# Attention and an expert MLP fused on one core: v of granule 1 loaded ahead of w_in, and its head's bias products, masks and scores rearranged

## The chip, the cores and the metric

One core of one Trainium2 chip. The time is the device time of one execution in microseconds (us). A program on one core has no second core to compare with, so a run counts as fast if it is within 1.5% of the fastest run of the same kernel; every run told here that could be classified was fast, at a granted TensorE clock of 0.992 to 1.0 (one experiment has a single run, whose state is unknown). The profile is of one execution; its span is some 2 us shorter than the device time.

Engines: PE = TensorE matmul, PEld = its weight load, DVE = VectorE, ACT = ScalarE, POOL = GpSimd, SP = SyncE.

## The reference, cut to what matters

```python
# q, k, v: (4 batches, 8 heads, 768 positions, 64), float32
scores = q @ k.T / sqrt(64)
keep   = (pos_k < 8) | ((0 <= pos_q - pos_k) & (pos_q - pos_k < 96))   # 8 global keys, window of 96
scores = where(keep, scores - slope[h] * dist, -1e9)
a      = softmax(scores) @ v                        # slope[h] = 2 ** -(h + 1)
x      = a as (3072 tokens, 512)
out    = (s * relu(x @ w_in) ** 2 + b) @ w_out      # w_in 512 x 2048, w_out 2048 x 512
```

## The kernel before: the parts concerned

The tokens are worked off in 12 granules of 256 (j below); three granules make a batch. P1(j, f) is the f-th of eight groups of eight matmuls of x @ w_in. P1(0, f) is the first user of piece f of w_in. S are the scores of a granule, A is attention times values, XT is the transposition of its result for P1. A comment marks what is cut.

A score can get its bias and its mask in two ways. Either PE adds the bias before the scores (SB_mm, one matmul per head with a scaled diagonal as weights, `biased=True`), or DVE multiplies the exponentials by exp(bias) afterwards (S_mul with tmpl). The second way needs ACT to have made tmpl. In the granules 0 and 1 everything goes the first way.

```python
    # all loads are issued by POOL, in this order
    load_v(0)
    load_quads(1, "k")
    load_quads(1, "q")
    load_w_in(0, 8)
    load_w_in(1, 8)
    load_v(1)
    for i in range(2, 8):
        load_w_in(i, 8)
    # ... k, q, v of granule 2, three pieces of w_out; later more_loads():
    #     k of 3, last piece of w_out, q of 3, v of 3, granule 4

    def SB_mm(j, hp, which=None):           # bias on PE
        # ...
        for hi in range(2):
            nc.tensor.matmul(
                ps[:, hi, 0:n], lhsT=diag[:, 2 * hp + hi, :], rhs=m, start=True, stop=False
            )

    def S_mul(j, hp):                       # mask on DVE
        # ...
            m = tmpl[:, 2 * hp : 2 * hp + 2, c0 : c0 + n]
            nc.vector.tensor_tensor(pt[:, :, 0:n], pt[:, :, 0:n], m, ALU.mult)

    # the order of the head, from granule 1 on
    SB_mm(1, 0)
    P1(0, 0, "dve", "pso")
    SB_mm(1, 1)
    S_mm(1, 0, True)
    S_post(1, 0, True)
    S_mm(1, 1, True)
    S_post(1, 1, True)
    P1(0, 1)
    SB_mm(1, 2)
    S_mm(1, 2, True)
    S_post(1, 2, True)
    VO(1)
    SB_mm(1, 3)
    S_mm(1, 3, True)
    S_post(1, 3, True)
    A(1, 0)
    A(1, 1, "pso")
    P1(0, 2)
    make_tmpl(0)
    make_tmpl(1)
    A(1, 2)
    P1(0, 3)
    A(1, 3, "pso")
    XT_half(1, 0, "act", "av")
    P1(0, 4)
    XT_half(1, 1, "dve", "pso")
    P1(0, 5)
    P1(1, 0)                                # from here PE streams
```

The softmax here doesn't subtract the row's maximum and nothing guards it: scores larger than these inputs give would overflow.

## Time and profile before

| | before |
|---|---|
| median of three runs | 208.09 us (208.04 to 208.14) |
| span of the profiled execution (a further one, 207.70 us) | 205.9 us |
| PE busy | 199.9 us, 97% |
| start of P1(0,0), P1(0,1), P1(0,2), P1(0,5) | 12.69, 14.66, 17.89, 21.44 us |
| landing of pieces 0, 1, 2, 5 of w_in | 12.04, 13.38, 17.13, 21.15 us |

A load is done by 16 DMA engines, and its completion comes in 16 parts. It has landed with the last part, and that is the time in the table. One view more is needed for the comparison, PE's timeline of the head (start, duration, instruction, count):

```profile
12.69 1.06 PE L528 MATMUL ps<-xT,w_in_bf 128*128 128x256 bf16 x8
...
14.66 1.05 PE L528 MATMUL ps<-xT,w_in_bf 128*128 128x256 bf16 x8
...
21.44 5.41 PE L528 MATMUL ps<-xT,w_in_bf 128*128 128x256 bf16 x48
```

P1(0,0) starts 0.65 us and P1(0,1) 1.3 us after its piece has landed. PE does not wait for pieces 0 and 1. The third line is the start of the stream, P1(0,5).

### The profile page before, as it was taken

Reading aid. Unit: us, or ns where it says so; the run is one execution under the profiler, and the core shown is the slowest. Engines: PE = TensorE matmul, PEld = TensorE weight load, DVE = VectorE, ACT = ScalarE, POOL = GpSimd, SP = SyncE. Lnnn points to the kernel's source line nnn. Section 1 sums busy time; section 2 is a strip of 40 time slices with the busy share of each in tenths; the row PEclk is TensorE's granted clock in tenths of the full one; section 3 lists DMA queues with packets and bytes.
Section 4 is the critical chain, followed back from the end, with each engine's and each line's share of the span. In section 5 each row is a group of like instructions: output and inputs, shape, how many; then the busy total and the mean of one; then the engine's idle time right before and its main releaser. Section 6 shows DMA issues by size and latency. Waiting matters only on the chain.

```text
span 205.9 us, 5605 instructions
## 1 busy us (share of the span) xinstructions
PE 199.9 (97%) x2291; PEld 161.0 (78%) x2299; DVE 169.1 (82%) x409; ACT 118.3 (57%) x181; POOL 73.7 (36%) x98
## 2 busy tenths in 40 slices
PE   7999999999999999999999999999999999999993
PEld 2667886547766678988988988988978988988883
DVE  3685576799989989788799799788799799787693
ACT  5779799455978586536446546546356446424400
POOL 8994673848273019009019029037000000000000
PEclk9999999999999999999999999999999999999999
DMA  5999999999999979999999969979946040050022
GB/s 165 194 183 198 190 194 193 182 148 162 134 125 155 211 112 102 188 159 129 190 128 106 208 82 117 204 114 119 194 80 178 3 135 21 0 153 3 2 105 102
DMA packets 103962, 27.64 MB, mean 134 GB/s; under 512 B 91392, under 2 KB 102016, under 8 KB 103936
## 3 DMA queue, kind: packets, MB, share of 16 engines
q0 software_dynamic: 70976, 13.11, 85.0%
q1 hardware_dynamic: 31904, 13.64, 34.2%
q10 hardware_dynamic: 1056, 0.52, 0.9%
q8 instruction: 18, 0.29, 0.6%
q14 instruction: 8, 0.07, 0.2%
HBM read 27.26 MB, written 6.29 MB: 163 GB/s over the span
## 4 chain that ended last, share of the span: by engine, by line
PE 83%; DVE 8%; ACT 3%; DMA 3%; issue 1%; POOL 0%; SPq 0%; DVEq 0%; ACTq 0%; POOLq 0%
PE ps L528 37%; PE ps_w L702 14%; PE ps_wb L702 6%; PE ps L589 6%; PE ps_av L446 5%; PE ps_s L395 5%; PE ps_wa L702 4%; ACT pt L408 2%; DMA raw<-in_k_dram 2%; PE ps_s L379 2%; DVE xn L464 2%; PE ps_2s L589 2%; DVE pt L418 2%; DMA xT<-xn 1%; DVE o_pr L627 1%
## 5 line engine op out<-in xcount | busy, mean ns | idle before, releaser
L528 PE MATMUL ps<-xT,w_in_bf 128*128 128x256 bf16 x768 | 96.6, 273 | 0.5 <-DVE xn L464 0.2
L528 PEld LDWEIGHTS <-w_in_bf 128*128 128x128 bf16 x768 | 72.7, 98 | 11.4 <-DVE xn L464 0.5
L540 ACT ACTIVATE gT<-ps 128x512 bf16<-128x512 f32 x72 | 43.1, 598 | 58.7 <-PE ps L528 55.9
L408 ACT ACTIVATE pt<-ps_s 128x1024 bf16<-128x1024 f32 (+1 forms) x48 | 43.1, 952 | 2.4 <-PE ps_s L395 2.4
L702 PEld LDWEIGHTS <-sw 128*128 128x128 bf16 x288 | 28.1, 98 | 3.4
L418 DVE TENSOR_TENSOR pt<-pt,tmpl 128x1024 bf16<-128x1024 bf16 (+1 forms) x40 | 25.1, 646 | 2.8 <-ACT pt L408 2.3
L556 DVE TENSOR_TENSOR gT<-gT 128x512 bf16<-128x512 bf16 x68 | 25.8, 415 | 1.8 <-ACT gT L540 1.6
L112 POOL DMA_DIRECT2D vaug<-in_v_dram x24 | 21.5, 913 | 3.9 <-DMA w_out_bf<-in_moe_w_out_dram 1.7
L702 PEld LDWEIGHTS <-gT 128*128 128x128 bf16 x208 | 19.7, 98 | 3.2 <-issue 0.2
L464 DVE TENSOR_TENSOR xn<-ps_av,rc 128x256 bf16<-128x256 f32 x48 | 20.4, 424 | 1.7
L125 POOL COPY pdum<-xT 1x1 bf16<-1x1 bf16 x5 | 3.0, 595 | 49.3 <-DMA xT<-xn 49.3
L589 PE MATMUL ps<-w_out_bf,gT 128*128 128x512 bf16 x74 | 18.8, 379 | 0.4 <-issue 0.2
L702 PE MATMUL ps_w<-tw,sw 128*128 128x256 bf16 x144 | 18.7, 273 | 0.0
L712 DVE SCALAR_TENSOR_TENSOR u<-ps_w,s_bc,bvec 128x256 f32<-128x256 f32 x27 | 12.9, 478 | 6.3 <-PE ps_w L702 6.3
L446 PEld LDWEIGHTS <-pt 128*128 128x128 bf16 x352 | 15.3, 98 | 3.6 <-DVE pt L418 1.2
L538 ACT ACTIVATE gT<-ps 128x512 bf16<-128x512 f32 x24 | 14.2, 599 | 5.1 <-PE ps L528 5.0
L104 POOL DMA_DIRECT2D qnat<-in_q_dram x18 | 16.0, 906 | 2.7 <-PE ps L528 1.8
L104 POOL DMA_DIRECT2D knat<-in_k_dram x18 | 15.9, 893 | 2.1 <-issue 1.6
L446 PE MATMUL ps_av<-vaug,pt 128*128 128x65 bf16 x224 | 16.4, 194 | 0.3 <-DVE pt L418 0.2
L463 DVE RECIPROCAL rc<-ps_av 128x4 f32<-128x4 f32 x48 | 8.7, 181 | 8.8 <-PE ps_av L446 8.5
L589 PEld LDWEIGHTS <-gT 128*128 128x128 bf16 x96 | 8.8, 98 | 8.1
L395 PE MATMUL ps_s<-qT,kT 64*128 64x128 bf16 x224 | 12.5, 218 | 0.0
(99 smaller groups left out, 240.8 us busy)
## 6 DMA issues: line engine op xcount, KB each, us to landing
out_dram<-o_pr SPq DMA_DIRECT2D x10, 512.0 KB, 5.9
vaug<-in_v_dram POOLq DMA_DIRECT2D x24, 128.0 KB, 7.9
knat<-in_k_dram POOLq DMA_DIRECT2D x22, 128.0 KB, 6.1
qnat<-in_q_dram POOLq DMA_DIRECT2D x22, 128.0 KB, 8.0
w_in_bf<-in_moe_w_in_dram POOLq DMA_DIRECT2D x8, 256.0 KB, 7.9
w_out_bf<-in_moe_w_out_dram POOLq DMA_DIRECT2D x4, 512.0 KB, 10.1
out_dram<-o_pr SPq DMA_DIRECT2D x3, 256.0 KB, 2.6
raw<-in_q_dram ACTq DMA_DIRECT2D x2, 256.0 KB, 4.8
```

Of the source, the lines that this page charges most:

```text
L104: nc.gpsimd.dma_start(t[:, i, :, :], src[b, :, sb * P : (sb + 1) * P, :].rearrange("h p d -> p h d"))
L112: nc.gpsimd.dma_start(vaug[b % 2][:, sb, :, 0:D], v[b, :, sb * P : (sb + 1) * P, :].rearrange("h p d -> p h d"),)
L395: nc.tensor.matmul(ps[:, hi, oc * P : (oc + 1) * P], lhsT=kt[r, :], rhs=qT[j][r, hp, i * P : (i + 1) * P], start=not biased, stop=not bias ...
L408: nc.scalar.activation(pt[:, :, 0:n], ps[:, :, 0:n], ACT.Exp, scale=QSCALE)
L418: nc.vector.tensor_tensor(pt[:, :, 0:n], pt[:, :, 0:n], m, ALU.mult)
L446: nc.tensor.matmul(av[:, i, hi, :], lhsT=pt[:, hi, c * P : (c + 1) * P], rhs=vv, start=n_ == 0, stop=n_ == len(ops) - 1,)
L464: nc.vector.tensor_tensor(xn[j][:, :, 2 * hp : 2 * hp + 2, :], av[:, :, :, 0:D], rc[:].to_broadcast((P, GB, 2, D)), ALU.mult,)
L528: nc.tensor.matmul(ps[:, i, :], lhsT=w_in_bf[:, kc, fc * P : (fc + 1) * P], rhs=xT[j][:, kc, :], start=(kc == 0), stop=(kc == KC - 1),)
L540: nc.scalar.activation(gs.rearrange("p f (r t) -> p f r t", r=2), ps[:].rearrange("p f (t r) -> p f r t", r=2), ACT.Relu,)
L556: nc.vector.tensor_tensor(gs, gs, gs, ALU.mult)
L589: nc.tensor.matmul(po[j, tb], lhsT=gT[j][:, fc, tb * P : (tb + 1) * P], rhs=w_out_bf[:, fc, :], start=(fc == 0), stop=(fc == FC - 1),)
L702: nc.tensor.matmul(wt[j, ps], lhsT=lhs[:, f, :], rhs=rhs[:, f, :], start=first and f == 0, stop=f == HF - 1, skip_group_check=True,)
```

## The change

Its intent, as the code shows it: take two of granule 1's four bias products off PE and put the work on DVE as masks, start granule 1's scores while the first piece of w_in is still under way, and have its v there early. The masks for the repeated block pattern are also made with fewer, longer ACT calls from a smaller table. The diff, cut to its core:

```diff
     load_quads(1, "q")
-    load_w_in(0, 8)
-    load_w_in(1, 8)
     load_v(1)
-    for i in range(2, 8):
+    for i in range(8):
         load_w_in(i, 8)
# ... diag (8 scaled diagonals) goes; bias (8 scaled copies of a 3-block base) comes,
#     and the bias product becomes ident x bias instead of diag x base
-    tmpl = const.tile([P, H, 5 * P], BF16, name="tmpl")
+    tmpl = const.tile([P, H, 3, P], BF16, name="tmpl")
# ... make_tmpl: four calls for several heads instead of eight for one
     def S_mul(j, hp):
+            m = m[:, :, 1:3, :].rearrange("p h a c -> p h (a c)")
+            x = pt[:].rearrange("p h (i c) -> p h i c", i=GB)
+            nc.vector.tensor_tensor(x, x, m.unsqueeze(2).to_broadcast((P, 2, GB, 2 * P)), ALU.mult)
# ... the head, from granule 1's first bias product on
     SB_mm(1, 0)
-    P1(0, 0, "dve", "pso")
-    SB_mm(1, 1)
+    XT_half(0, 1, "dve", "psh")
+    T_ev(1, 1, "q", "act")
+    T_ev(1, 1, "k")
+    KO_own(1)
+    VO(1)
     S_mm(1, 0, True)
     S_post(1, 0, True)
-    S_mm(1, 1, True)
-    S_post(1, 1, True)
-    P1(0, 1)
-    SB_mm(1, 2)
-    S_mm(1, 2, True)
-    S_post(1, 2, True)
-    VO(1)
+    S_mm(1, 1)
+    S_post(1, 1, mul=False)
+    P1(0, 0, "late", "pso", relu="dve")
+    S_mul(1, 1)
+    S_mm(1, 2)
+    S_post(1, 2, mul=False)
+    P1(0, 1, "late", relu="dve")
     SB_mm(1, 3)
     S_mm(1, 3, True)
     S_post(1, 3, True)
-    A(1, 0)
-    A(1, 1, "pso")
-    P1(0, 2)
-    make_tmpl(0)
-    make_tmpl(1)
-    A(1, 2)
-    P1(0, 3)
-    A(1, 3, "pso")
+    S_mul(1, 2)
+    P1(0, 2, "late")
# ... A(1,0), A(1,1), P1(0,3), A(1,2), A(1,3), each normalised apart
     XT_half(1, 0, "act", "av")
-    P1(0, 4)
+    P1(0, 4, "late")
     XT_half(1, 1, "dve", "pso")
+    for f in range(5):
+        Q(0, f)                             # the five squares that were put off
     P1(0, 5)
```

## The prediction

> **What bounds the kernel now.** I read the page first, then the chain that ended last, then the timeline of the first 25 us.
>
> ```profile
> span 205.9 us, 5605 instructions
> PE 199.9 (97%) x2291; PEld 161.0 (78%) x2299; DVE 169.1 (82%) x409; ACT 118.3 (57%) x181; POOL 73.7 (36%) x98
> PE   7999999999999999999999999999999999999993
> PE 83%; DVE 8%; ACT 3%; DMA 3%; issue 1%; POOL 0%; SPq 0%; DVEq 0%; ACTq 0%; POOLq 0%
> ```
>
> PE is 97% busy and carries 83% of the chain. Only the first slice (5.1 us) has idle PE to speak of, yet the change touches almost only the first 35 us. So the question is when PE reaches the point from which it only streams. In the chain in order of time that point is the eight-matmul groups of the first MLP product (L528, called P1(granule, pair) below):
>
> ```profile
> 17.46 0.59 PE ps_av L446 x16
> 18.05 0.87 PE ps L528 x8
> 19.17 0.87 PE ps L528 x8
> 20.51 0.87 PE ps L528 x8
> 21.61 5.24 PE ps L528 x48
> ```
>
> P1(0,2), P1(0,3), P1(0,4) come one by one, then P1(0,5) starts a run of 48. Pair f needs piece f of w_in. When the pieces land is seen on POOL, which issues the loads; it has eight landing semaphores in rotation, so each issue waits for the load issued eight before it:
>
> ```profile
> 6.96 1.51 POOL L129 DMA_DIRECT2D w_in_bf<-in_moe_w_in_dram  x2
> 8.43 1.79 POOL L112 DMA_DIRECT2D vaug<-in_v_dram  x2
> 10.17 4.50 POOL L129 DMA_DIRECT2D w_in_bf<-in_moe_w_in_dram  x6
> ...
> 16.20 0.61 POOL L92 DMA_DIRECT2D knat<-in_k_dram  x1 [0.86 <-DMA vaug<-in_v_dram]
> 17.42 0.61 POOL L92 DMA_DIRECT2D qnat<-in_q_dram  x1 [0.60 <-DMA w_in_bf<-in_moe_w_in_dram]
> 18.80 0.61 POOL L92 DMA_DIRECT2D qnat<-in_q_dram  x1 [0.77 <-DMA w_in_bf<-in_moe_w_in_dram]
> 20.10 0.90 POOL L112 DMA_DIRECT2D vaug<-in_v_dram  x1 [0.69 <-DMA w_in_bf<-in_moe_w_in_dram]
> 21.43 0.88 POOL L112 DMA_DIRECT2D vaug<-in_v_dram  x1 [0.44 <-DMA w_in_bf<-in_moe_w_in_dram]
> ```
>
> The four issues at 17.42, 18.80, 20.10 and 21.43 wait for pieces 2, 3, 4 and 5. Asked one by one for their time to landing (7.0, 7.6, 8.2, 8.8 us, issued 0.73 us apart from 10.17), these pieces land at 17.15, 18.5, 19.8 and 21.15; pieces 0 and 1 at 12.05 and 13.4 (5.1 and 5.7 us after issue). PE starts P1(0,2..5) at 17.9, 19.0, 20.3 and 21.44: it runs only 0.75, 0.5, 0.5 and 0.3 us behind the arrivals. PE looks like the bound here, but w_in stands right behind it.
>
> One more thing delays these arrivals. The DMA view of 13.5 to 14.7 us has
>
> ```profile
> q8 instruction: 1, 0.02, 5.0%
> ```
>
> one instruction fetch: 5.0% of 16 engines over 1.2 us, so 0.96 us of one engine. One sixteenth of every load then comes late: the second v load, due 0.83 us after the first (14.25), is complete only at 15.9, and the pieces behind it inherit some 0.75 us. Eighteen such fetches in the kernel against some 4,600 PE instructions is one in about 256, so a fetch comes at a place in PE's program, not at a time.
>
> **What the Trainium skill says.** "TensorE: Matmul & The Clock Gate", section "Wait — 56ns, not 53.3ns?", gives a warm matmul N / 2.4 GHz + 2.5 ns from start to start: 109 ns for 256 columns, 216 for 512. The trace agrees (0.87 us for 8). "VectorE: DVE Perf Modes", section "What auto-detection actually checks": 16-bit operands with step ±1 take the two-element mode. The mask multiplication of 1024 elements takes 685 ns here, where (1024/2 + 151)/0.96 gives 691; the trace agrees for the old pattern, and an outer stride of zero does not break the stated condition. That the same copy with a repeated source block takes as long (426 against 430 ns, the two copies of vo) supports it. "ScalarE: Activation LUTs", section "What ACT_TABLE_LOAD costs": 186 + 0.833·N ns; the 1024-element exponentials take 1,025 ns (1,039 by that). "DMA: Bandwidth & Descriptors", section "Queues, rings and completion order": an engine takes descriptors of one ring in order. The trace agrees: loads land in the order of issue, so moving the v loads ahead makes two pieces of w_in later by exactly these loads.
>
> **The change, part by part.**
>
> *PE.* Head pairs 1 and 2 of granule 1 lose their bias product: 2 × 2 × 216 ns = 0.87 us. The instruction order shows 4,592 rows instead of 4,600, and the second granule's scores for pairs 0 and 1 now stand before P1(0,0), pair 2 between P1(0,0) and P1(0,1). All else on PE is the same work.
>
> *DVE.* In: two mask multiplications of 0.685, two ReLUs from PSUM of about 0.69 (estimate from the 0.42 us of the 128x256 normalisation, which also reads PSUM), six bias tables of 384 elements, about 0.2 each (estimate from 0.125 for 128). Out: four diagonals (0.50), two base copies. The tables fall into DVE's 1.28 us wait for q before 4.83, and the rest is about 2.7 us between 15 and 18, where DVE now idles 2.2 us. The five late squares merely move to 22 to 25 us, where DVE is half busy. Nothing of this is on the path.
>
> *ACT.* Eight masks of 640 (8 × 0.751) become four calls, two of 1024 and two of 512: 5.6 down to about 3.3 us. One of 1024 goes into ACT's 0.96 us wait before 5.96; about 1.03 long, it delays the first q copy by at most 0.1 us, and PE is still in bias products until 6.6. Off the path.
>
> *Loads.* v of granule 1 before w_in. From the last q load (11.07) to the second v load the stream delivers two pieces of w_in (1.34 us each) and two v loads (0.85 each, of which about 0.97 for the first after q), 4.0 us in all. In the new order piece 1 stands last of these four, so it is due at 15.1, and piece 0 at 13.75. The fetch comes at about the 360th PE row, which after the change is reached about half a microsecond earlier, around 13.1; it hits piece 0. So I take piece 0 at 14.5 and piece 1 at 15.9. Pieces 2 to 7 stay where they are.
>
> *The head of PE anew.* Scores of pairs 0 and 1: q transposed by 11.8, evacuated on ACT by 13.0, so done by 13.35 (before: 14.7). Then P1(0,0) waits for piece 0: 14.5. It ends 15.4; scores of pair 2 with two changes of matmul shape 0.47; P1(0,1) at 15.9, just with piece 1; end 16.8. Bias product 0.44 and scores 0.47 of pair 3: P1(0,2) at 17.75, piece 2 long there. From here before had P1, A, P1, A, transposes, P1, transposes = 3 × 0.87 + 2 × 0.245 + 2 × 0.22 = 3.54 (17.9 + 3.54 = 21.44, as measured). After, all four A (attention times values) stand there: 4.04. P1(0,5) at 17.75 + 4.04 = 21.8, against 21.44. So +0.35 us: the 0.87 us saved on PE, and the earlier scores, turn into a wait of 1.2 us for piece 0. From P1(0,5) on the stream is the same, PE is full to the end, and the shift goes through. Gaps downstream (summing PE starts, under 1 us between 33 and 77) may absorb 0.1.
>
> Sum: 208.09 + 0.35 - 0.1 = 208.3 us.
>
> **Rivals.** (1) The saving comes through. For it: PE has no gaps in the head worth the name after 12.5. Against: P1(0,5) cannot start before piece 5 lands at 21.15, and no load order changes what lies before that piece. That caps the gain at 0.3 us: 207.8. It needs the fetch to come after piece 1. (2) The repeated table drops the mask multiplication to one element a cycle: 28 calls become 1.22 us, 28 × 0.53 = 15 us more on an engine that is busy 169 of 206; perhaps 214 to 218. Against: the skill's condition, and the vo copies. (3) ACT relief shortens 33 to 40 us, where three masks run on ACT before the exponential at 36.59. Against: that exponential waited for PE (0.33 from the scores), and the two remaining masks take as long there; 0.1 us. (4) ReLU and multiplication on DVE make the last two A wait: their masks are done by about 18.2, needed at 20; nothing.
>
> **Range and chances.** The two outcomes of the arrivals, -0.3 and +0.45, with some absorption and 0.3 us for what I mis-time, give 207.5 to 208.9. A change of 2% is 4.2 us: only rival 2 reaches it, and nothing gains that much in a head already paced by w_in. Faster 0.01, same 0.97, slower 0.02.
>
> **What would show it.** In the timeline after: scores of granule 1 before 13.5; then PE idle for about 1 us ahead of the first L528-like group, released by the w_in load; P1(0,5) at 21.8 (at 21.2 rival 1 holds); a mask multiplication of 0.69, not 1.2 us. If piece 0 is there by 13.8 and piece 1 by 15.1, I have the fetch wrong; if the shift at P1(0,5) and the shift at the end differ by over 0.3 us, the later stream isn't rigid.

## The result, and the profile after

| | before | after | predicted |
|---|---|---|---|
| median of four runs each, same chip, alternating | 208.06 us (207.65 to 208.14) | 207.81 us (207.59 to 208.13) | 208.3 (207.5 to 208.9) |
| ratio of fast runs | | 0.9993 (95%: 0.9974 to 1.0012) | |
| the same once more, other chip (the last below) | 207.5 us | 207.82 us; 1.0009 (0.9996 to 1.0022) | |
| span | 205.9 | 205.9 | |

A ratio here is the mean time of one kernel's fast runs over that of the other's of the same rounds, so it is not quite the ratio of the medians quoted. The two kernels are equal: one comparison has the changed kernel 0.25 us ahead, the other 0.32 us behind, and both intervals hold 1. The page of the changed kernel, beside the page lines in the prediction:

```profile
span 205.9 us, 5606 instructions
PE 199.8 (97%) x2295; PEld 160.8 (78%) x2295; DVE 172.9 (84%) x415; ACT 115.6 (56%) x173; POOL 73.7 (36%) x98
PE 84%; DMA 4%; POOL 4%; DVE 4%; ACT 1%; issue 0%; SPq 0%; POOLq 0%
```

PE is as busy as before although it lost four products. ACT lost 2.7 us and DVE gained 3.8 us, and neither shows in the span. What did change in the chain that ended last is its beginning. In order of time it now holds (start, duration, engine, what):

```profile
9.48 6.50 DMA w_in_bf<-in_moe_w_in_dram
16.03 1.05 PE ps L552 x8
17.84 0.98 PE ps L552 x8
...
21.99 5.32 PE ps L552 x48
```

The load of piece 1 of w_in, issued at 9.48, lies on the path, where before PE's own work led to P1(0,2). PE's timeline of the same stretch, to be laid beside the three lines of before (L552 is P1, L414 the scores; brackets: idle time just before, and what ended it):

```profile
13.84 1.05 PE L552 MATMUL ps<-xT,w_in_bf 128*128 128x256 bf16 x8
14.82 0.29 PE L414 MATMUL ps_s<-qT,kT 64*128 64x128 bf16 x4
...
16.03 1.05 PE L552 MATMUL ps<-xT,w_in_bf 128*128 128x256 bf16 x8 [0.81 <-DMA w_in_bf<-in_moe_w_in_dram]
...
17.77 1.05 PE L552 MATMUL ps<-xT,w_in_bf 128*128 128x256 bf16 x8
...
21.89 3.34 PE L552 MATMUL ps<-xT,w_in_bf 128*128 128x256 bf16 x29
```

PE is idle 0.81 us ahead of P1(0,1): that is where the 0.87 us of saved bias products went. P1(0,5) comes at 21.89, 0.45 us later than before. (The count of 29 is only where the window asked for ends.) The DMA view of 13.4 to 15.0 us says why piece 1 is late:

```profile
q8 instruction: 1, 0.02, 3.8%
```

One fetch of PE instructions starts at 13.63 and holds one of the 16 DMA engines; 3.8% of 16 engines over 1.6 us is 0.97 us. Fifteen parts of piece 1 are there at 15.09 or before, the sixteenth at 15.98. A second fetch at 19.73 does the same to piece 5: fourteen of its parts came by 20.4, the last two at 21.27 and 21.85. And the mask multiplication with the repeated table, in the page's groups (count | busy us, mean ns):

```profile
L441 DVE TENSOR_TENSOR pt<-pt,tmpl 128x1024 bf16<-128x1024 bf16 x30 | 20.0, 685 | 1.8 <-ACT pt L427 1.8
```

685 ns, as before.

**Where the 0.45 us went.** Starts of the same P1 matmul in both traces, and later in the experiments, as differences to before:

| P1 matmul number (start before, us) | after | after, second profile | e1 | e2 | e9 | e10 | e11 |
|---|---|---|---|---|---|---|---|
| 40: P1(0,5) (21.44) | +0.45 | +0.69 | +0.50 | +1.26 | +0.01 | -1.15 | +0.16 |
| 88: P1(0,7) (27.16) | +0.45 | +0.68 | +0.50 | +1.25 | +0.01 | -1.16 | +0.15 |
| 120 (31.91) | +0.35 | +0.57 | +0.40 | +1.26 | -0.10 | -1.27 | +0.07 |
| 136 (47.98) | +0.22 | +0.44 | +0.27 | +1.27 | -0.23 | -1.40 | +0.93 |
| 160 (52.88) | +0.22 | +0.43 | +0.26 | +1.26 | +1.27 | +0.24 | +0.92 |
| 300 (86.54) | +0.23 | +0.44 | +0.28 | +1.28 | +1.29 | +0.27 | +0.93 |
| 600 (158.64) | -0.03 | +0.19 | +0.02 | +1.07 | +1.17 | 0.00 | +0.77 |

Two steps take the shift back. The first, 0.23 us between 27 and 48 us, is partly seen. In before, ACT makes a mask at 26.51 just when it should copy transposed k, and the second batch of transposes has to wait for it; after, that mask is gone. PE's timelines, before and then after:

```profile
28.13 0.55 PE L288 MATMUL ps_t<-ident,qnat 64*64 64x64 bf16 x32
```
```profile
28.59 0.45 PE L287 MATMUL ps_t<-ident,qnat 64*64 64x64 bf16 x32
```

That is 0.10 us. The rest is several waits under 0.1 us for DVE and ACT between 31 and 37 us that are shorter after the change. The second step, 0.26 us, is a wait in the kernel before. PE's timeline of before:

```profile
152.87 1.05 PE L702 MATMUL ps_w<-w_out_bf,gT 128*128 128x256 bf16 x8
154.01 1.03 PE L528 MATMUL ps<-xT,w_in_bf 128*128 128x256 bf16 x8
```

Eight such matmuls go out in 0.87 us, so the P1 that follows was due at 153.74, and it starts at 154.01. It needs x transposed, and that transfer took 4.3 us instead of 2.4. The source view of these transfers from 147 to 150 us, before and then after:

```profile
DMA to landing us min/median/max: 2.4/3.3/4.3
```
```profile
DMA to landing us min/median/max: 2.4/2.4/2.5
```

An instruction fetch at 151.53 ran while it was in flight. Nothing in the code of the change touches this place, but the change takes eight instructions (four matmuls and their weight loads) out of PE's program ahead of it. All fourteen traces agree that this decides. In the six whose program has the old number of instructions (before, e2, e3, e4, e5, e7) the fetch starts at 151.5 to 151.8, if the shift of PE's work is taken off, and the last part of the second transfer lands 1.6 to 2.0 us after the fifteenth. In the eight others the fetch starts at 151.9 or later, or, with 54 instructions more (e8), at 150.3, and this transfer is on time. P1 waits for the late part only as far as it is due before it: 0.26 us in before, 0.37 in e5, and next to nothing in e3, where the part lands at 153.94 and P1 was due at about 154.0. So this step is an effect of the change, but of where the fetch falls and not of the work saved.

### The profile page after: what moved, and what is told of

Same layout as the page of the kernel before. It is cut to its first block, busy times and chain, and to the rows that moved or that the text cites. A ratio compares the mean times of both kernels' runs of the same rounds, so it can differ in the third digit from the quotient of the medians.

```text
span 205.9 us, 5606 instructions
## 1 busy us (share of the span) xinstructions
PE 199.8 (97%) x2295; PEld 160.8 (78%) x2295; DVE 172.9 (84%) x415; ACT 115.6 (56%) x173; POOL 73.7 (36%) x98
## 4 chain that ended last, share of the span: by engine, by line
PE 84%; DMA 4%; POOL 4%; DVE 4%; ACT 1%; issue 0%; SPq 0%; POOLq 0%
PE ps L552 38%; PE ps_w L728 15%; PE ps L615 7%; PE ps_wb L728 7%; PE ps_av L470 4%; PE ps_s L414 4%; PE ps_wa L728 4%; DMA w_in_bf<-in_moe_w_in_dram 3%; POOL vaug L112 2%; PE ps_2s L615 2%; DMA xT<-xn 1%; DVE pt L441 1%; DVE o_pr L653 1%; POOL qnat L92 1%; POOL knat L92 1%; ACT gT L566 1%
## 5 line engine op out<-in xcount | busy, mean ns | idle before, releaser
L552 PE MATMUL ps<-xT,w_in_bf 128*128 128x256 bf16 x768 | 96.5, 273 | 1.2 <-DMA w_in_bf<-in_moe_w_in_dram 0.8
L552 PEld LDWEIGHTS <-w_in_bf 128*128 128x128 bf16 x768 | 72.6, 98 | 12.1 <-DMA w_in_bf<-in_moe_w_in_dram 1.1
L566 ACT ACTIVATE gT<-ps 128x512 bf16<-128x512 f32 x72 | 43.1, 598 | 58.5 <-PE ps L552 56.4
L582 DVE TENSOR_TENSOR gT<-gT 128x512 bf16<-128x512 bf16 x73 | 27.6, 416 | 1.7 <-ACT gT L566 1.6
L488 DVE TENSOR_TENSOR xn<-ps_av,rc 128x256 bf16<-128x256 f32 x48 | 20.4, 424 | 1.7
L441 DVE TENSOR_TENSOR pt<-pt,tmpl 128x1024 bf16<-128x1024 bf16 x30 | 20.0, 685 | 1.8 <-ACT pt L427 1.8
L615 PE MATMUL ps<-w_out_bf,gT 128*128 128x512 bf16 x80 | 19.7, 379 | 0.0
L104 POOL DMA_DIRECT2D qnat<-in_q_dram x18 | 15.9, 901 | 2.8 <-DMA w_out_bf<-in_moe_w_out_dram 1.4
L564 ACT ACTIVATE gT<-ps 128x512 bf16<-128x512 f32 x22 | 13.0, 598 | 6.1 <-PE ps L552 5.9
L414 PE MATMUL ps_s<-qT,kT 64*128 64x128 bf16 x224 | 12.5, 218 | 0.1
```

Of the source, the lines that this page charges most:

```text
L104: nc.gpsimd.dma_start(t[:, i, :, :], src[b, :, sb * P : (sb + 1) * P, :].rearrange("h p d -> p h d"))
L414: nc.tensor.matmul(ps[:, hi, oc * P : (oc + 1) * P], lhsT=kt[r, :], rhs=qT[j][r, hp, i * P : (i + 1) * P], start=not biased, stop=not bias ...
L441: nc.vector.tensor_tensor(x, x, m.unsqueeze(2).to_broadcast((P, 2, GB, 2 * P)), ALU.mult)
L488: nc.vector.tensor_tensor(xn[j][:, :, 2 * hp : 2 * hp + 2, :], av[:, :, :, 0:D], rc[:].to_broadcast((P, GB, 2, D)), ALU.mult,)
L552: nc.tensor.matmul(ps[:, i, :], lhsT=w_in_bf[:, kc, fc * P : (fc + 1) * P], rhs=xT[j][:, kc, :], start=(kc == 0), stop=(kc == KC - 1),)
L566: nc.scalar.activation(gs.rearrange("p f (r t) -> p f r t", r=2), ps[:].rearrange("p f (t r) -> p f r t", r=2), ACT.Relu,)
```

## The experiments

Twelve kernels were run; e1 to e4, e5 to e8, e9 with e10, and e11 with e12 each shared a chip and its runs of before. The diffs are against the kernel named. Starts are from PE's timelines, landings from the loads' completion parts.

| run | time, us (range, runs) | ratio to before (95%) | P1(0,0) | P1(0,1) | P1(0,5) |
|---|---|---|---|---|---|
| e1 | 207.62 (207.16-207.71, 6) | 0.9981 (0.9967-0.9994) | 13.33 | 14.64 | 21.94 |
| e2 | 208.91 (208.76-209.27, 4) | 1.0048 (1.0031-1.0065) | 13.89 | 16.04 | 22.70 |
| e3 | 207.91 (207.75-208.20, 4) | 0.9999 (0.9983-1.0015) | 14.35 | 16.09 | 21.89 |
| e4 | 207.92 (207.79-208.11, 4) | 0.9999 (0.9981-1.0017) | | | 21.52 |
| e5 | 207.82 (207.64-208.20, 4) | 0.9985 (0.9965-1.0005) | 13.05 | | 21.81 |
| e6 | 206.98 (206.21-208.06, 4) | 0.9951 (0.9910-0.9993) | 15.07 | 16.38 | 22.18 |
| e7 | 207.83 (207.64-209.77, 4) | 1.0009 (0.9962-1.0057) | 14.82 | 16.15 | 21.98 |
| e8 | 207.95 (one run) | | 15.03 | 16.36 | 22.16 |
| e9 | 209.19 (207.62-209.94, 6) | 1.0046 (1.0010-1.0082) | 13.21 | 14.51 | 21.45 |
| e10 | 207.22 (206.72-208.11, 4) | 0.9964 (0.9925-1.0003) | 13.18 | 14.49 | 20.29 |
| e11 | 209.02 (208.54-209.32, 6) | 1.0065 (1.0051-1.0079) | 13.67 | 14.98 | 21.60 |
| e12 | 207.82 (207.75-207.90, 5) | 1.0009 (0.9996-1.0022) | 13.88 | 16.33 | 22.13 |

My theory was that the arrivals of w_in pace the head, so that PE's saving becomes a wait and the new order of loads costs. The rivals: the saving is real and comes through, or PE and the other engines pace the head and the loads don't matter.

### e1: the changed kernel with the old order of loads

```diff
     load_quads(1, "q")
+    load_w_in(0, 8)
+    load_w_in(1, 8)
     load_v(1)
-    for i in range(8):
+    for i in range(2, 8):
         load_w_in(i, 8)
# and VO(1), which needs v, moved from before S_mm(1, 0, True) to after P1(0, 1)
```

> The changed kernel with the old order of loads (two pieces of w_in, then v of granule 1) and the copy of v moved behind the second ReLU on DVE; the result stays correct. Theory 1, the arrivals of w_in pace the head: the wait of 0.81 us before the second P1 group goes; P1(0,1) starts at 15.1 to 15.3 instead of 16.03, P1(0,2) at 17.2 (piece 2), P1(0,5) at 21.3 to 21.5 instead of 21.89; the time falls by 0.3 to 0.6 us against the changed kernel, to 207.3 to 207.5. Theory 2, the load order doesn't matter because PE's own work sets the head: P1(0,5) stays at 21.9 and the time at 207.8.

The wait for piece 1 went, as it should: P1(0,1) starts at 14.64. PE's timeline of this kernel:

```profile
14.64 1.05 PE L554 MATMUL ps<-xT,w_in_bf 128*128 128x256 bf16 x8
...
17.25 1.05 PE L554 MATMUL ps<-xT,w_in_bf 128*128 128x256 bf16 x8 [0.80 <-DMA w_in_bf<-in_moe_w_in_dram]
...
21.94 1.27 PE L554 MATMUL ps<-xT,w_in_bf 128*128 128x256 bf16 x10 [0.45 <-ACT gT L566]
```

The wait moved on to piece 2, which lands at 17.20, and then to piece 5. The last line names ACT, the release that came last by the profile's reckoning. But piece 5 lands only at 21.90, because this time the second fetch (19.87) hits it, and POOL's issue that waits for piece 5 goes out late too:

```profile
22.18 0.88 POOL L112 DMA_DIRECT2D vaug<-in_v_dram  x1 [1.12 <-DMA w_in_bf<-in_moe_w_in_dram]
```

P1(0,5) at 21.94 misses what I expected there by half a microsecond, for that fetch; the median, 207.62, lies 0.1 us above the expected range. From P1(0,2) to P1(0,5) it takes 4.69 us here, and 4.06 to 4.12 in all other traces of the changed head (after, e3, e6 to e12), which confirms that piece 5 held it. With the new order of loads or the old, one of the pieces is late by the same fetches, and P1(0,5) is at 21.9. By the time, e1 is the best kernel that still does the whole work: 0.19% ahead of before, with an interval that leaves out 1. That is little more than the 0.16% by which the two comparisons of the changed kernel itself differ (0.9993 and 1.0009).

### e2: the kernel before with the new order of loads only

The same edit of load_w_in and load_v as in the change, nothing else.

> The kernel before with nothing but v of granule 1 moved ahead of w_in. Theory 1: its PE order has P1(0,0) ahead of three quarters of granule 1's scores, so it waits at P1(0,0) until piece 0 lands (13.8 instead of 12.69) and at P1(0,1) until piece 1 (16.0 instead of 14.66); P1(0,5) at about 22.8 instead of 21.44; time 209.0 to 209.4. Theory 2: PE catches up within the head, P1(0,5) within 0.3 us of 21.44, time 208.0 to 208.3.

The order of loads by itself costs 0.48%, 1.0 us: P1(0,0) starts at 13.89, right after piece 0 (13.84), P1(0,1) at 16.04 after piece 1 (15.99), and the shift of +1.26 at P1(0,5) stays to 134 us. The rival that loads do not matter is out. It follows too that the rest of the change, under the new order, earns about 0.8 of these 1.26 us back (P1(0,5) from 22.70 to 21.89).

### e3: the changed kernel with all four bias products on PE

```diff
-    S_mm(1, 1)
-    S_post(1, 1, mul=False)
+    SB_mm(1, 1)
+    S_mm(1, 1, True)
+    S_post(1, 1, True)
     P1(0, 0, "late", "pso", relu="dve")
-    S_mul(1, 1)
-    S_mm(1, 2)
-    S_post(1, 2, mul=False)
+    SB_mm(1, 2)
+    S_mm(1, 2, True)
+    S_post(1, 2, True)
# and without S_mul(1, 2)
```

> The changed kernel with the bias products of pairs 1 and 2 put back on PE and their two mask multiplications taken off DVE; everything else, loads too, as changed. Theory 1: the 0.87 us of PE work go into the waits before P1(0,0) and P1(0,1); P1(0,1) starts at 16.0 to 16.2, P1(0,5) at 21.9 to 22.0, the time within 0.15 us of the changed kernel's 207.8. Theory 2: P1(0,5) 0.5 us or more later, time 208.4 or more.

PE has 0.87 us more to do in the head and P1(0,5) is at 21.89, to the hundredth as without. The saved products are worth nothing here: they fill the wait for piece 1 (P1(0,1) at 16.09 against 16.03). So what brings P1(0,5) from 22.70 in e2 to 21.89 is not the masks but the rest of the rearrangement, of which the scores of granule 1 ahead of the first piece of w_in are the part that the timeline shows; no run takes this rest apart.

### e4: the kernel before with one mask made earlier

```diff
     P1(0, 5)
+    make_tmpl(2)
     P1(1, 0)
...
     P1(1, 3)
-    make_tmpl(2)
     P1(0, 6)
```

> The kernel before with one of its mask exponentials on ACT (the third) made 4 us earlier, ahead of the granule's first P1(1,0) and not just before the transposes of granule 2. If ACT's relief is what gives back 0.10 us at the second block of transposes of granule 2 (28.13 to 28.62 in the kernel before, 0.55 long against 0.45), that block now takes 0.45 and all PE groups from 28.6 on are 0.10 us earlier; the time is 0.1 us lower, too little to tell by time. If not, the block stays 0.55 long.

From P1(0,7) to the fifth P1 of granule 1 it takes 1.36 us instead of 1.46 (27.45 to 28.81): the 0.10 us of ACT relief is confirmed at its place. The mask costs 0.2 us where it now stands (P1(0,5) to P1(0,7) 5.93 instead of 5.72 us), so the time can't tell. In this trace a fetch at 14.09 made piece 5 land at 21.48, and P1(0,5) came right behind it, 1.27 us after P1(0,4) instead of 1.09: here w_in holds the kernel before too, by some 0.2 us.

### e5 and e6: both kernels without the v loads of granule 1

```diff
+    nc.vector.memset(vaug[0][:, 2:4, :, 0:D], 0.0)
# and without load_v(1)
```

The result is wrong, zeros for a third of batch 0's v. The comparison passed both all the same, since v's share stays within the tolerance, so "correct" says little for these rows.

> The kernel before without the two loads of v for granule 1 (zeros instead, made on DVE at the start: wrong on purpose), so that each piece of w_in from piece 2 on lands some 1.7 us earlier. The head of this kernel should be bound by PE alone: P1(0,5) at 21.4 to 21.5 as in the kernel before, time unchanged, 207.9 to 208.2. If the arrivals already held it, P1(0,5) would come earlier.

> The changed kernel without the two loads of v for granule 1 (zeros instead, wrong on purpose), so that all pieces of w_in land some 1.7 us earlier. Theory 1 (arrivals hold the changed head): no wait before P1(0,1), which starts at 15.0 to 15.3; P1(0,5) at 20.8 to 21.1, 0.4 to 0.6 us ahead of the same edit to the kernel before, and time 0.6 to 0.9 us below it, near 207.2. Theory 2: P1(0,5) stays at 21.7 to 21.9 with the loads out of the way.

In e5 P1(0,0) to P1(0,5) takes 8.76 us against 8.75 in before, although the pieces come earlier (piece 5 at 19.57 instead of 21.15): the head of the kernel before is paced by PE, not by w_in. P1(0,5) itself, at 21.81, missed the expected 21.4 to 21.5, because this execution was 0.36 us late already at P1(0,0). In e6 the same stretch takes 7.11 us against 8.05 (13.84 to 21.89). Without v in the way PE is what is left in the changed head, and there the saving is real. The execution of e6 that was profiled had a late start (its raw loads landed 0.37 to 0.39 us later than in after, and its first matmuls ran slow), which is why its absolute starts missed; e10 repeats it.

### e7 and e8: the changed kernel with more PE instructions ahead

```diff
-    idle(9, "av")          # nine warming matmuls of 512 columns
+    idle(5, "av")
+    idle(8, "av", 2 * P)   # e7: the same columns, 4 matmuls and so 8 PE instructions more
# e8: idle(36, "av", P), 54 PE instructions more
```

> The changed kernel with eight more PE instructions in the idle loop at the start (five matmuls of 512 columns and eight of 256 instead of nine of 512: the same columns), so that from there on each PE instruction has the place in the program that it has in the kernel before. If the instruction fetches follow the place in PE's program, and the fetch at 151.5 is what made the transposed activations of one granule late in the kernel before (a wait of 0.26 us at 153.7 which the changed kernel doesn't have), the wait comes back here and the time rises by about 0.25 us to 208.0 to 208.1. If that wait is an accident of one execution, nothing changes.

> The changed kernel with 54 more PE instructions in the idle loop (36 matmuls of 128 columns instead of nine of 512). If the fetch follows the place in PE's program, the first comes at 11.8 to 12.3 instead of 13.63 and hits piece 0 of w_in: P1(0,0) starts at 14.4 to 14.7 instead of 13.84, as was predicted for the changed kernel; P1(0,1) still at 16.0 and P1(0,5) at 21.8 to 21.9. If fetches come by time, P1(0,0) stays at 13.8.

I had counted a fetch to come at a place in PE's program, about once in 256 instructions, and predicted that it hits piece 0. With eight instructions more it does: the fetch is at 11.86 instead of 13.63, piece 0 lands at 14.78 and piece 1 at 16.11. PE's timeline of e7:

```profile
14.82 1.05 PE L552 MATMUL ps<-xT,w_in_bf 128*128 128x256 bf16 x8 [1.26 <-DMA w_in_bf<-in_moe_w_in_dram]
...
16.15 1.05 PE L552 MATMUL ps<-xT,w_in_bf 128*128 128x256 bf16 x8
...
21.98 1.26 PE L552 MATMUL ps<-xT,w_in_bf 128*128 128x256 bf16 x10
```

The wait is now before P1(0,0), and P1(0,1) and P1(0,5) are where they were, within 0.12 us. Whether the fetch hits piece 0 or piece 1 does not matter: the delayed DMA engine works its parts off in order, so piece 1 is late either way. e8, with a fetch at 11.47, shows the same order of events, but everything comes later than I expected: pieces 0 and 1 land at 14.99 and 16.31, and P1(0,0), P1(0,1) and P1(0,5) start 0.3 us above their ranges.

What e7 was built for, the wait at 153.7 us, came back as well: the last part of the transfer lands at 154.11, and P1 waits 0.18 us. The profiled execution took 208.01 us, as expected, but the median of the four, 207.83, lies below the range, and one of them took 209.77.

### e9: the old order of loads and 32 PE instructions fewer

To e1's edit it adds transposes of granule 0 that take two heads at once, so that the second fetch comes behind piece 5:

```diff
-                for hi in range(2):
-                    nc.tensor.transpose(
-                        ps[hi * D : (hi + 1) * D, a, e, i * P : (i + 1) * P],
-                        nat[nm, j][:, 4 * half + 2 * e + hi, i * D : (i + 1) * D],
-                        ident[:],
-                    )
+                h = 4 * half + 2 * e
+                nc.tensor.transpose(
+                    ps[:, a, e, i * P : (i + 1) * P],
+                    nat[nm, j][:, i, h : h + 2, :],
+                    ident[:],
+                )
```

> The changed kernel with the old load order (as e1_old_loads) and 32 PE instructions fewer ahead of granule 1: the 32 transposes of granule 0 that make 64 columns each become 16 of 128, their input written by the casts in the order that this needs. Correct. In e1_old_loads piece 5 of w_in landed at 21.90 because the second fetch, at 19.87, hit it, and P1(0,5) started at 21.94. With 32 instructions fewer that fetch should come at 20.2 or later, piece 5 at 21.2, P1(0,5) at 21.2 to 21.4, and the time 0.4 to 0.7 us below e1_old_loads, 206.9 to 207.2. If fetches don't follow the place in the program, or piece 5 isn't what holds P1(0,5), it starts at 21.9 as before and the time stays at 207.6.

The head did as expected: the second fetch at 21.27, piece 5 at 21.35, P1(0,5) at 21.45. But the time rose. The table of differences shows the place: -0.23 us at 48 us, +1.27 us at 53 us. In between stand the scores of granule 3, whose q comes through a load and then a transposing transfer; PE's waits from 45 to 55 us:

```profile
PE ps_s L417 <- DMA qT<-qnat: 1.3, 1, 1.3
```

Transposed q landed at 51.98. In before it landed at 50.27, and the scores started at 50.70, with 0.43 us to spare. So there is a second barrier behind the head, with 0.43 us to spare in before. That q came 1.7 us late in e9 is another matter. The loads ahead of it were late already: the first of k of granule 3 landed at 38.31 instead of 37.10, the last piece of w_out at 41.72 instead of 40.50, each by its last parts. In e1, with the same order of loads, they were on time (37.11 and 40.52). Why they were late in this execution is open; two of the six runs took 207.62 and 208.03 us.

### e10: the changed kernel without the v loads, again

> The same kernel as e6_after_no_v1, whose four times spread from 206.21 to 208.06 and whose profiled execution was the slowest of them, with the first loads 0.35 us late and the first matmuls at half rate until 9 us. Theory: with the arrivals out of the way nothing absorbs such a late start, so it shows in the time. In an execution with a start like that of the changed kernel (S of granule 1 at 12.7 to 13.0) P1(0,0) starts at 13.7 to 13.9, P1(0,1) at 15.0 to 15.2 without a wait and P1(0,5) at 20.7 to 21.0, and the time is 206.2 to 206.8. P1(0,0) to P1(0,5) takes 7.1 us whatever the start.

This time the start was good, even 0.4 to 0.5 us better than the ranges expected, while the median, 207.22, lies above its range: P1(0,5) at 20.29, again 7.11 us after P1(0,0), and 1.15 us earlier than in before. PE's timeline at granule 3's scores:

```profile
49.30 0.23 PE L414 MATMUL ps_s<-qT,kT 64*128 64x128 bf16 x2
51.00 0.46 PE L414 MATMUL ps_s<-qT,kT 64*128 64x128 bf16 x10 [1.47 <-DMA qT<-qnat]
```

The head start is waited away there, and behind it the kernel is 0.24 us behind before. Even a head without any v in the way would not show in this trace. But here too the loads were late: the last piece of w_out landed at 40.11 and transposed q at 50.96, while e6, the same program, had them at 38.75 and 48.65 and no such wait. Two of the runs (206.72 and 206.73, and 206.21 and 206.46 in e6) are 1 to 2 us faster than before's median all the same; their traces were not taken, so this stays open.

### e11: e9 with q of granule 3 loaded ahead of the last piece of w_out

```diff
     def more_loads():
         load_rows(3, "k")
-        load_w_out(3)
         load_rows(3, "q")
+        load_w_out(3)
         load_v(3)
```

> The kernel of e9 (old load order, fewer transposes), with the q of granule 3 loaded ahead of the last piece of w_out instead of behind it. Theory (second barrier): in e9 P1(0,5) came at 21.45, 0.44 us earlier than in the changed kernel, but the scores of granule 3 waited 1.3 to 1.5 us at 50.5 us for their transposed q, which landed at 51.98. Expected: transposed q lands 1.2 to 2.6 us earlier, at 49.4 to 50.8; granule 3's scores start at about 50.5 with a wait below 0.4 us; the last w_out piece lands about 1.3 us later (43.0 instead of 41.7) and may cost up to 0.5 us there; P1(0,5) at 21.3 to 21.6; time 206.9 to 207.4 in the fast state. Rival (the transposed q is late for another reason than the place of its load in the queue, such as the transposing transfer's own queue): it still lands near 52, the wait stays above 1 us, and the time is that of e9, 207.6 to 209.9.

Transposed q landed at 50.64, and the scores of granule 3 did not wait (51.62). But the last piece of w_out landed at 43.68 instead of 41.72, and PE's timeline shows the wait in its new place:

```profile
43.72 1.89 PE L618 MATMUL ps<-w_out_bf,gT 128*128 128x512 bf16 x8 [0.82 <-DMA w_out_bf<-in_moe_w_out_dram]
...
51.62 0.51 PE L417 MATMUL ps_s<-qT,kT 64*128 64x128 bf16 x12
```

This speaks against the rival (the place in the queue isn't the reason): with the new place the second load of q landed at 40.97 instead of 44.48, and transposed q 1.3 us earlier. The 1.3 us alone would prove little, since two executions of one program, e6 and e10, differ by 2.3 us in this landing. My expected time is refuted too: I had allowed 0.5 us for w_out and it took 0.82 (+0.07 to +0.93 in the table), and 209.02 us is 0.65% above before. The profiled span is only 0.8 us over that of before, so about half of the 1.5 us in the medians is not in the trace, and I cannot say where it is. I do not count it as shown.

### e12: the changed kernel again

> The changed kernel unchanged, on the same chip as e11, to give e11 a direct comparison and to see how far a second profiled execution of the same program differs. Expected: 207.6 to 208.0, P1(0,0) at 13.7 to 14.5, P1(0,5) at 21.8 to 22.0, ratio to the kernel before 0.998 to 1.001. If the gain of 0.25 us in medians is only scatter, the ratio's interval holds 1; if the accidental wait of the kernel before at 153.6 us explains it, this profile again shows no wait there.

The first fetch comes at 14.21 here and again hits piece 1 (fifteen parts by 15.1, the last at 16.28); P1(0,1) waits 1.07 us and starts at 16.33. The second fetch at 20.26 misses piece 5 this time (21.32), and P1(0,5) is at 22.13 nevertheless. From P1(0,1) on it is 5.80 us, against 5.86 in the first profile and 5.83 in e7. So it is piece 1, and then PE's own work, that sets P1(0,5) in the changed kernel; the late piece 5 of the first profile cost 0.06 us at most (P1(0,4) to P1(0,5) 1.17 us there, 1.10 here). P1(0,5) came 0.13 us later than the range I had given, since piece 1 landed 0.3 us later (16.28 against 15.98). The end shows the two executions 0.22 us apart, and no wait at 153.6 in either.

## Why the prediction was right or wrong

**Right: arrivals take the place of PE's work.** The step "the 0.87 us saved on PE, and the earlier scores, turn into a wait" holds. After the change PE idles ahead of P1(0,1), released by w_in; e2 shows the price of the load order (1.0 us) and e3 that the saved products buy nothing. P1(0,1) was predicted at 15.9, P1(0,2) at 17.75 and P1(0,5) at 21.8; measured were 16.03, 17.77 and 21.89.

**Right for before: PE is the bound there.** e5 shows it directly (8.76 against 8.75 us). What I called "w_in stands right behind it" is true as well: one change of order, and it is in front; in e4 a fetch alone put it there.

**Wrong: which piece the fetch hits.** The step was "reached about half a microsecond earlier, around 13.1; it hits piece 0. So I take piece 0 at 14.5". The fetch came at 13.63, the time of before, and hit piece 1: piece 0 landed at 13.79 and P1(0,0) started at 13.84, not 14.5. The wait of 1.2 us that I had put before P1(0,0) was not there: the scores, which I had done by 13.35, ended only at 13.85, and the wait was 0.81 us before P1(0,1). The error had no consequence, and e7 shows why: eight instructions more give my picture to within 0.32 us, with the same P1(0,5). The delay belongs to one DMA engine and stays with all its parts that follow, so piece 1 at 15.9 was safe to within 0.4 us whichever piece was hit (15.98 to 16.31 in after, e7, e8 and e12). The condition that I had written for it ("If piece 0 is there by 13.8 and piece 1 by 15.1") came half true, 13.79 for the one and 15.98 for the other. Between the two pieces is just where the fetch struck.

The Trainium skill has the mechanism ("Runtime: NRT & Kernel Launch", section "Instruction fetch mechanics"): instructions are refilled in blocks of 16 KiB, which hold 256 instructions, by the sequencer's own DMA queue, at a cost that it calls "mostly hidden". I had worked that out from the trace and not looked there. The traces agree with the size (0.02 MB for one fetch, 18 fetches in all before). What the traces show beside it is that a load which shares the DMA engine is late, piece 1 by 0.9 us in one profile and 1.2 us in the other.

**Wrong: "Pieces 2 to 7 stay where they are".** Piece 5 came at 21.85 instead of 21.15, since the second fetch moved from 20.27 to 19.73. e12 shows that this was not what set P1(0,5), but for 0.06 us. In e1 it was.

**Mis-sized: the absorption.** The sum was 208.09 + 0.35 - 0.1. The first term was +0.45 in one trace and +0.69 in the other, the second 0.23 to 0.25 by 48 us, of which 0.10 is ACT's relief (e4) and the rest small waits. "From P1(0,5) on the stream is the same, PE is full to the end, and the shift goes through" is right from 48 to 151 us (+0.22 to +0.23) and wrong before and after. What the prediction named as its test, a shift at P1(0,5) and at the end that differ by over 0.3 us, came true: +0.45 against -0.03. The later stream is not rigid. One loss in it, 0.26 us at 153.7 us, is the kernel before's own: a fetch there makes a transposing transfer late in all six traces with the old number of PE instructions and in none of the eight others. The change lost it by taking eight instructions out, wherever they stood. That is luck of placement, which neither the change nor I had in view.

**The rivals.** The dropped mode of DVE (rival 2) is refuted with 685 ns. The saving that comes through (rival 1, P1(0,5) at 21.2) did not occur; its cap, piece 5 at 21.15, was itself not fixed. The third rival's 0.1 us was right in size; it was ACT's copy of transposed k that was freed, though, not an exponential. The fourth was right to within 0.1 us: from P1(0,2) to P1(0,5) it took 4.12 us for the 4.04 that I had summed. I did not see at all that granule 3's scores have only 0.43 us to spare in before. In the profiles of e9 and e10, where the loads ahead were late as well, the gain of the head was lost there, and e11 moved the wait to w_out; in e6 nothing was lost there. How much of a faster head would come through is open.

**Slips in the working.** The 0.97 us that I gave to the first v load after q belongs to piece 0 of w_in (11.07 to 12.04); the sum of 4.0 us is right. The formula with 151 cycles does not stand in the section that I named but in the same page's section "The TRN2 errata — SBUF-src ops pay a fixed extra latency per instruction", for additions in float32; to use it with half the elements was an estimate, which the 685 ns bear out to 1%.

**By the time.** The predicted middle, 208.3, is 0.5 us above the measured 207.81. The same-chip differences of after and before, -0.25 and +0.32 us, straddle zero, so +0.2 can be neither confirmed nor excluded; it is below what these runs resolve. That the outcome was "same" says little by itself: 2% is 4.2 us, and only rival 2 would have reached that.

## What to carry to other kernels

When loads on one queue follow each other without a gap and PE follows closely behind, work taken off PE turns into a wait unless the next arrival comes earlier too; and moving loads ahead makes others late by their length (the two v loads made piece 0 land at 13.79 instead of 12.04). Before hoping for a gain in the head, look for the next place where a transfer lands just in time: here granule 3's q had 0.43 us to spare at 50 us, and in two profiles (e9, e10) it came too late. An edit that changes the number of instructions moves the later fetches, and with them which transfers come late; look for that before crediting the edit's work with a few tenths of a microsecond. Take two profiles of the same program before explaining differences of a quarter of a microsecond: the two of this kernel differ by 0.24 us at P1(0,5).

## What the Trainium skill lacked or had wrong

- "Runtime: NRT & Kernel Launch", section "Instruction fetch mechanics" calls the block refill mostly hidden. It lacks that the refill takes about 0.96 us of one of the DMA engines that carry the loads, so that a load which is waited for is complete late (piece 1: fifteen parts by 15.09, the last at 15.98; in e12 by 15.12 and at 16.28), and that the number of instructions ahead decides which transfer is hit (at 152 us one transfer is 1.6 to 2.0 us late in all six traces with one number of instructions, and on time in the eight with others).
- "DMA: Bandwidth & Descriptors", section "Queues, rings and completion order" has the order within a ring (for the queues of SP and ACT; the loads here are POOL's), but not its consequence for loads in a row: the delay of one engine is handed on, so piece 1 lands at 15.98 and 16.28 where it is hit itself (after, e12) and at 16.11 and 16.31 where the piece before it is (e7, e8).
- "VectorE: DVE Perf Modes", section "The TRN2 errata — SBUF-src ops pay a fixed extra latency per instruction", gives 120 cycles and one per element at 0.96 GHz for a source in PSUM, by which a ReLU of 512 elements would take an estimated 658 ns; here it takes 679 ns, 3% more.
